# A fused retention and feed-forward kernel on one core: two units' casts and transposes moved ahead of later loads, and more zero matmuls at the start

## The chip, the core and the metric

The kernel runs on one core of a Trainium2 chip. A core has five engines, each with its own stream of instructions executed in order: TensorE (PE) for matmuls, VectorE (DVE), ScalarE (ACT), GpSimd (POOL) and SyncE (SP), which here only issues DMA transfers. Engines wait for each other and for transfers by semaphores. The metric is the device time of one execution in microseconds (us); lower is better.

## The reference

Inputs are q, k and v of shape (8 batches, 8 heads, 576 positions, 64) and two weight matrices, all float32.

```
scores = (q @ k^T) / sqrt(64)
D[h,i,j] = gamma[h] ** (i - j) if i >= j else 0      # gamma[h] = 1 - 2 ** (-5 - h)
attn = (scores * D) @ v
x = attn with heads side by side                      # 4608 tokens x 512
h = x @ w_in                                          # 512 x 2048
out = max(0.01 * h, h) @ w_out                        # 2048 x 512
```

So it is a decaying, causal linear attention with no softmax, followed by a two-layer feed-forward with a leaky rectifier, for 4608 tokens.

## The kernel before

**Two levels of tiling.** The attention works on 36 *units* of 128 tokens, each two chunks of 64. The feed-forward works on 18 *groups* of 256 tokens. Everything that goes into a matmul is float16; sums are float32 in PSUM.

**One unit.** Its k, q and v arrive by three loads of 256 KB (`loads`, L151; six half loads where a unit spans two batches). `casts(u)` (L180) makes float16 of them: `cast_k` is one ACT instruction (L157); `cast_q` and `cast_v` multiply by the decay table (L160), on DVE for units below 6 and on POOL from 6 on. Scores need q and k with the head dimension on the partitions. For units below 7, `transposes` (L187) does that with eight PE transposes and two copies out of PSUM; from unit 7 on, `cast_q` itself issues a DMA transpose from SP (L171), which reads `qk16` in SBUF and writes `qkT` in SBUF. `scores(u)` (L209) then computes the masked block's scores (L216) and the k-v products (L225) into the only `sc` PSUM tile; `masks` (L232) and `states` (L241) read it on DVE and so free it for the next unit; `state_copy` makes float16 of the state, on ACT below unit 8 and on POOL above. `outputs(u)` (L313) multiplies scores and state by v and q (L323, L334), and ACT (L342) and DVE (L346) bring the sum into `xT`.

**One group.** `g1_blocks` (L442) makes the hidden layer in eight blocks: eight matmuls of 256 columns (L454) into one of two `hps` PSUM buffers, and one ACT activation (L461), which frees the buffer. `g2_blocks` (L468) does the second layer: two token blocks of 16 matmuls of 512 columns (L477), copied out by DVE (L487) and stored by SP (L489). `g2_wide` (L508) does the same for groups 0 and 1.

**What sets the order.** The program text is each engine's order; nothing is rescheduled. The beginning is written out by hand (L542 to L654): units 0 to 7 with their casts and the first three groups' blocks between them. After that, `steady(n)` (L406) is one step: scores of unit n, outputs of n-1, masks, states, casts of n+3, and loads of n+7. `run` (L497) spreads these steps evenly between the blocks of one group's first layer and the previous group's second, so that a step's small matmuls come every few blocks.

**Queues.** Until unit 11, loads are issued by POOL, which also does casts; `ring` (L128) makes POOL wait so that only so many bytes are in flight. From unit 12 on, SP issues the loads. SP's queue thus holds, in program order, the DMA transposes, the loads from unit 12 on, and the stores of the result. Each tile of a pool has a fixed number of buffers: five for loads, six for casts and transposes.

**Zero matmuls.** `keep_warm(n)` (L377) issues n matmuls of 128x512 on a tile of zeros (L381) into an `hps` buffer that nothing reads; it stands after the PE transposes of the first units. `small_ones(60)` (L383) does it with 64x64 matmuls before the first data arrive.

Of the kernel before, what the change touches and what calls it, by code (L numbers as in the profile page):

```python
# [17 lines left out]
def kernel(  # L18
# [23 lines left out]
    nc = tc.nc  # L42
# [16 lines left out]
    NU = NT // P  # L59
# [78 lines left out]
    def load(u, x, eng):  # L138
        t = ld_pool.tile([P, H, D], FP, name=f"t32_{x}")
        t32[u, x] = t  # L140
        (b0, c0), (b1, c1) = units[u]
        src = (q, k, v)[x]
        parts = [(t, b0, c0, P)] if b0 == b1 else [(t[0:CH], b0, c0, CH), (t[CH:P], b1, c1, CH)]
        for dst, b, c, n in parts:
            if eng is nc.gpsimd:
                ring(H * n * D * 4, dst[0:1, 0, 0:1])
            eng.dma_start(  # L147
                out=dst, in_=src[b, :, CH * c : CH * c + n, :].rearrange("h t d -> t h d")
            )

    def loads(u, eng):  # L151
        for x in (1, 0, 2):
            load(u, x, eng)

    def cast_k(u):
        qk16[u] = b_pool.tile([P, 2, H, D], F16, name="qk16")
        nc.scalar.copy(out=qk16[u][:, 1], in_=t32[u, 1])  # L157

    def scaled(u, x, out):
        (nc.vector if u < NEARLY else nc.gpsimd).tensor_tensor(  # L160
            out=out,
            in0=t32[u, x],
            in1=tab_sb[:, kind(u), x // 2, :].unsqueeze(2).to_broadcast([P, H, D]),
            op=MUL,
        )

    def cast_q(u):
        scaled(u, 0, qk16[u][:, 0])
        if u >= NPE:
            qkT[u] = b_pool.tile([P, 2, NP, P], F16, name="qkT")  # L170
            nc.sync.dma_start_transpose(  # L171
                out=qkT[u].rearrange("p x c t -> p (x c) t"),
                in_=qk16[u].rearrange("t x h d -> t (x h d)"),
            )

    def cast_v(u):
        v16[u] = b_pool.tile([P, H, D], F16, name="v16")
        scaled(u, 2, v16[u])

    def casts(u):  # L180
        if u >= NU:
            return
        cast_k(u)
        cast_q(u)
        cast_v(u)

    def transposes(u, pool=None):  # L187

        qkT[u] = b_pool.tile([P, 2, NP, P], F16, name="qkT")
        if pool is None:  # L190
            trs = [y_pool.tile([P, NP, P], F16, name="yps") for x in range(2)]
        else:
            both = pool.tile([P, 2, 2 * NP, P], F16, name="sc" if pool is sc_pool else "ot")
            trs = [both[:, x, 0:NP, :] for x in range(2)]
        for x in (1, 0):
            for p in range(NP):
                nc.tensor.transpose(  # L197
                    trs[x][:, p, :],
                    qk16[u][:, x, 2 * p : 2 * p + 2, :].rearrange("t h d -> t (h d)"),
                    ident,  # L200
                )
        for x in (1, 0):
            (nc.scalar.copy if x or u < 4 else nc.vector.tensor_copy)(
                out=qkT[u][:, x], in_=trs[x]
            )
# [3 lines left out]
    def scores(u):  # L209

        a = sc_pool.tile([P, 2, 2, NP, CH], FP, name="sc")
        sc_tiles[u] = a
        for p in range(NP):
            for g in range(2):
                for j in range(2):
                    nc.tensor.matmul(  # L216
                        out=a[half(j), g, 0, p, :],
                        lhsT=qkT[u][half(g), 1, p, half(j)],
                        rhs=qkT[u][half(g), 0, p, half(j)],
                        start=True, stop=True, skip_group_check=True,  # L220
                    )
        for p in range(NP):
            for j in range(2):
                for g in range(2):
                    nc.tensor.matmul(  # L225
                        out=a[half(g), j, 1, p, :],
                        lhsT=qk16[u][half(j), 1, 2 * p + g, :],
                        rhs=v16[u][half(j), 2 * p + g, :],
                        start=True, stop=True, skip_group_check=True,
                    )  # L230

    def masks(u):  # L232
        s16s[u] = a_pool.tile([P, 2, NP, CH], F16, name="s16")
        nc.vector.tensor_tensor(  # L234
            out=s16s[u],
            in0=sc_tiles[u][:, :, 0],
            in1=mask_sb.unsqueeze(1).unsqueeze(1).to_broadcast([P, 2, NP, CH]),
            op=MUL,
        )

    def states(u, copy=True):  # L241

        st = sc_tiles[u][:, :, 1]
        s32 = a_pool.tile([P, 2, NP, CH], FP, name="s32")
        st32[u] = s32
        for j, (b, c) in enumerate(units[u]):
            if c == CB - 1:
                continue
            ends_block = c % CPB == CPB - 1
            dst = st[:, j] if ends_block else s32[:, j]  # L250
            if c == 0:
                nc.vector.tensor_copy(out=dst, in_=st[:, j])
            else:
                prev = s32[:, 0] if j else st32[u - 1][:, 1]
                nc.vector.tensor_tensor(out=dst, in0=st[:, j], in1=prev, op=ADD)  # L255
            if ends_block:
                nc.vector.tensor_tensor(
                    out=s32[:, j], in0=dst,
                    in1=gblk_sb.unsqueeze(2).to_broadcast([P, NP, CH]), op=MUL,
                )  # L260
        if copy:
            state_copy(u)
# [50 lines left out]
    def outputs(u):  # L313


        ot = ot_pool.tile([P, 2, 2 * NP, CH], FP, name="ot")
        own = ot[:, :, 0:NP]
        far = ot[:, :, NP : 2 * NP].rearrange("q r (s j) t -> q r s (j t)", j=2)
        for hp in range(NP):
            for h in (hp, hp + NP):  # L320
                o, c = divmod(h, NP)
                for j in range(2):
                    nc.tensor.matmul(  # L323
                        out=own[half(o), j, c, :],
                        lhsT=v16[u][half(j), h, :],
                        rhs=s16s[u][half(j), h % 2, h // 2, :],
                        start=True, stop=True, skip_group_check=True,
                    )
        for j in range(2):
            for s in range(2):  # L330
                for o in range(2):
                    for g in range(2):
                        p = 2 * o + s
                        nc.tensor.matmul(  # L334
                            out=far[half(o), g, s, half(j)],
                            lhsT=st_before(u, j)[half(g), p, :],
                            rhs=qkT[u][half(g), 0, p, half(j)],
                            start=True, stop=True, skip_group_check=True,
                        )
        t0 = P * u % XR  # L340
        tmp = a_pool.tile([P, NP, P], FP, name="own")
        nc.scalar.copy(  # L342
            out=tmp.rearrange("q c (j t) -> q c j t", t=CH),
            in_=own.rearrange("q j c t -> q c j t"),
        )
        nc.vector.tensor_tensor(  # L346
            out=xT[:, :, t0 : t0 + P].rearrange("q (s g) t -> q g s t", g=2),
            in0=far,
            in1=tmp.rearrange("q (s g) t -> q g s t", g=2),
            op=ADD,  # L350
        )
# [25 lines left out]
    def keep_warm(n):  # L377

        t = h_pool.tile([P, 1, TOK], FP, name="hps")
        for _ in range(n):  # L380
            nc.tensor.matmul(out=t[:, 0, :], lhsT=idle[:, 0:P], rhs=idle, start=True, stop=True)  # L381
# [24 lines left out]
    def steady(n):  # L406
        def go():
            if n < NU:
                scores(n)
            if n > NFIRST:  # L410
                outputs(n - 1)
            if n < NU:
                masks(n)
                states(n)
            casts(n + 3)
            if n + 7 < NU:
                loads(n + 7, nc.sync)

        steps.append((n - 1, go))

# [129 lines left out]
    states(0)  # L550
    cast_q(1)
    cast_v(1)
    transposes(1)
    keep_warm(1)
    cast_k(2)
    cast_q(2)
    scores(1)
# [44 lines left out]
    def more(blocks, a, b):  # L602
        for m in range(a, b):
            blocks[m]()
# [32 lines left out]
    more(g1[2], 3, 5)  # L637
    state_copy(6)
    casts(9)
    loads(12, nc.sync)  # L640
    more(g1[2], 5, 7)
    outputs(6)
    scores(7)
# [2 lines left out]
    more(g1[2], 7, 8)  # L646
    more(g2, 0, 1)
    state_copy(7)
    casts(10)
    loads(13, nc.sync)  # L650
    loads(14, nc.sync)
    more(g2, 1, 4)
    outputs(7)
    more(g2, 4, 6)  # L654
# [48 lines left out]
```

## Time and profile before

| | us |
|---|---|
| median of 6 runs | 309.73 (307.28 to 311.18) |
| the profiled execution: its own time | 311.39 |
| its span, first to last instruction | 309.6 |
| time until unit 3's first hidden-layer block on PE | 19.47 |
| DVE, ACT and POOL busy | 107.1, 137.8, 123.2 |
| PE: hidden layer (L454), second layer (L477) busy | 148.1, 128.0 |

The profile is of one execution. A row such as `L454 PE MATMUL hps<-xT,w_in` names the line in the kernel, the engine, the operation, and the tile written and those read. PEld is PE's loading of weights, beside its matmuls. SPq is SP's queue of issued transfers: the time given there is that of the issue, not of the transfer. A number in brackets is the engine's idle time just before an instruction, with what ended it. PEclk is the share of PE's full clock that was granted. The longest waits in total are of engines that follow PE:

```profile
ACT gt L461 <- PE hps L454: 130.0, 133, 2.4
DVE xT L346 <- ACT own L342: 83.9, 32, 6.3
DVE osb L487 <- PE yps L477: 75.6, 17, 6.3
POOL st L268 <- DVE s L255: 56.3, 12, 7.4
```

(Columns: who waited for whom, us in total, times, the longest.) These are waits of engines with time to spare. What PE itself waits for is small in sum, and has to be looked for by place:

```profile
PE yps L197 <- DVE qk L160: 3.0, 2, 1.6
PE sc L216 <- DMA qkT<-qk: 2.9, 1, 2.9
...
PE sc L216 <- DVE s L255: 1.2, 1, 1.2
```

### The profile page before, as it was taken

The page shows a single profiled execution, that of the slowest core. Times are in us where ns is not written, and L with a number is a line of the kernel's source. Part 1 is how long each engine was busy: PE and PEld are TensorE (multiplying, and loading weights), DVE is VectorE, ACT ScalarE, POOL GpSimd, SP SyncE. Part 2 cuts the span into 40 slices and gives each one's busy share as a digit, 9 for nine tenths or more (in the row PEclk, how much of TensorE's full clock was granted, in tenths as well). Part 3 has the DMA queues.
Part 4 walks back from the last instruction along what each step waited for, and adds up shares of the span by engine and source line. Part 5 has one row for each costly group of instructions (what it writes and reads, how often), then busy time and mean ns, then how long its engine had stood idle before and what let it go on. Part 6 is the DMA issues. An engine that isn't in the chain of part 4 may idle for free.

```text
span 309.6 us, 9470 instructions
## 1 busy us (share of the span) xinstructions
PE 295.9 (96%) x4164; PEld 199.9 (65%) x4164; DVE 107.1 (35%) x200; ACT 137.8 (45%) x240; POOL 123.2 (40%) x177
## 2 busy tenths in 40 slices
PE   4799999998699999999999999999999999999996
PEld 3468755856456666666666666766666666666663
DVE  2732035345223234333434234333334234332101
ACT  3556634846324444444444444444444444343320
POOL 8977969956333332433233333333333330000000
PEclk9999999999869999999999999999999999999999
DMA  8999997999999976887697967676873220000011
GB/s 227 248 195 229 206 274 215 227 240 204 239 209 247 238 166 170 131 212 174 170 154 186 173 174 168 173 179 173 147 199 82 78 70 36 36 36 34 36 65 70
DMA packets 120440, 50.26 MB, mean 162 GB/s; under 512 B 109264, under 2 KB 113744, under 8 KB 120400
## 3 DMA queue, kind: packets, MB, share of 16 engines
q1 hardware_dynamic: 112912, 36.38, 52.6%
q0 software_dynamic: 7056, 13.11, 18.1%
q8 instruction: 32, 0.52, 0.8%
q10 hardware_dynamic: 432, 0.17, 0.3%
q14 instruction: 8, 0.07, 0.1%
HBM read 36.81 MB, written 9.44 MB: 149 GB/s over the span
## 4 chain that ended last, share of the span: by engine, by line
PE 92%; DMA 3%; DVE 2%; issue 1%; ACT 1%; SPq 0%; POOL 0%; POOLq 0%; ACTq 0%; DVEq 0%
PE hps L454 39%; PE yps L477 35%; PE sc L216 3%; PE yps L522 2%; PE hps L522 2%; PE sc L225 2%; PE ot L323 2%; DMA t<-in_q_dram 2%; PE ot L334 1%; DMA qkT<-qk 1%; PE yps L663 1%; PE yps L197 1%; PE hps L381 1%; PE ot L290 1%; DVE s L234 1%
## 5 line engine op out<-in xcount | busy, mean ns | idle before, releaser
L454 PE MATMUL hps<-xT,w_in 128*128 128x256 f16 x1152 | 148.1, 275 | 0.0
L461 ACT ACTIVATE gt<-hps 128x512 f16<-128x512 f32 x144 | 85.8, 597 | 130.4 <-PE hps L454 130.0
L454 PEld LDWEIGHTS <-w_in 128*128 128x128 f16 x1152 | 113.1, 99 | 39.6 <-issue 1.6
L477 PE MATMUL yps<-w_out,gt 128*128 128x512 f16 x496 | 128.0, 384 | 0.0
L268 POOL CAST st<-s 128x512 f16<-128x512 f32 (+1 forms) x28 | 15.6, 556 | 144.0 <-DVE s L255 56.3
L477 PEld LDWEIGHTS <-gt 128*128 128x128 f16 x496 | 46.6, 98 | 35.1 <-issue 1.1
L346 DVE TENSOR_TENSOR xT<-ot,own 128x512 f16<-128x512 f32 x32 | 22.1, 692 | 83.9 <-ACT own L342 83.9
L487 DVE COPY osb<-yps 128x512 f32<-128x512 f32 x31 | 21.3, 687 | 75.6 <-PE yps L477 75.6
L160 POOL TENSOR_TENSOR qk<-t,cs 128x512 f16<-128x512 f32 x30 | 31.3, 1043 | 0.1
L160 POOL TENSOR_TENSOR v<-t,cs 128x512 f16<-128x512 f32 x30 | 31.2, 1042 | 0.0
L234 DVE TENSOR_TENSOR s<-sc,cs 128x512 f16<-128x512 f32 x36 | 24.6, 683 | 10.6 <-PE sc L225 10.6
L342 ACT COPY own<-ot 128x512 f32<-128x512 f32 x32 | 18.7, 585 | 11.9 <-PE ot L334 9.9
L157 ACT CAST qk<-t 128x512 f16<-128x512 f32 x36 | 22.3, 621 | 1.0 <-DMA t<-in_k_dram 1.0
L216 PEld LDWEIGHTS <-qkT 64*64 64x64 f16 x576 | 8.0, 111 | 14.0 <-issue 8.0
L255 DVE TENSOR_TENSOR s<-sc,s 128x256 f32<-128x256 f32 x40 | 16.8, 420 | 0.7
L216 PE MATMUL sc<-qkT 64*64 64x64 f16 x576 | 11.9, 203 | 4.3 <-DMA qkT<-qk 2.9
L147 POOL DMA_DIRECT2D t<-in_v_dram x13 | 11.3, 871 | 0.8 <-POOLq L687 0.8
L225 PE MATMUL sc<-v,qk 64*64 64x64 f16 x576 | 11.3, 198 | 0.0
L147 POOL DMA_DIRECT2D t<-in_q_dram x12 | 10.2, 853 | 2.1 <-DMA t<-in_k_dram 2.1
L147 POOL DMA_DIRECT2D t<-in_k_dram x12 | 10.4, 865 | 1.1 <-DMA t<-in_k_dram 1.1
L522 PEld LDWEIGHTS <-gt 128*128 128x128 f16 x64 | 5.9, 98 | 6.3
L323 PE MATMUL ot<-s,v 64*64 64x64 f16 x512 | 9.9, 195 | 0.0
(52 smaller groups left out, 147.8 us busy)
## 6 DMA issues: line engine op xcount, KB each, us to landing
out_dram<-osb SPq DMA_DIRECT2D x35, 256.0 KB, 3.5
t<-in_k_dram SPq DMA_DIRECT2D x22, 256.0 KB, 3.6
t<-in_q_dram SPq DMA_DIRECT2D x22, 256.0 KB, 3.9
t<-in_v_dram SPq DMA_DIRECT2D x21, 256.0 KB, 4.4
t<-in_v_dram POOLq DMA_DIRECT2D x11, 256.0 KB, 5.0
t<-in_k_dram POOLq DMA_DIRECT2D x10, 256.0 KB, 5.1
t<-in_q_dram POOLq DMA_DIRECT2D x10, 256.0 KB, 5.1
w_in<-in_moe_w_in_dram POOLq DMA_DIRECT2D x8, 256.0 KB, 6.9
```

The lines of the kernel that those rows point to most:

```text
L147: eng.dma_start(out=dst, in_=src[b, :, CH * c : CH * c + n, :].rearrange("h t d -> t h d"))
L157: nc.scalar.copy(out=qk16[u][:, 1], in_=t32[u, 1])
L160: (nc.vector if u < NEARLY else nc.gpsimd).tensor_tensor(out=out, in0=t32[u, x], in1=tab_sb[:, kind(u), x // 2, :].unsqueeze(2).to_broadca ...
L216: nc.tensor.matmul(out=a[half(j), g, 0, p, :], lhsT=qkT[u][half(g), 1, p, half(j)], rhs=qkT[u][half(g), 0, p, half(j)], start=True, stop=T ...
L234: nc.vector.tensor_tensor(out=s16s[u], in0=sc_tiles[u][:, :, 0], in1=mask_sb.unsqueeze(1).unsqueeze(1).to_broadcast([P, 2, NP, CH]), op=MUL,)
L342: nc.scalar.copy(out=tmp.rearrange("q c (j t) -> q c j t", t=CH), in_=own.rearrange("q j c t -> q c j t"),)
L346: nc.vector.tensor_tensor(out=xT[:, :, t0 : t0 + P].rearrange("q (s g) t -> q g s t", g=2), in0=far, in1=tmp.rearrange("q (s g) t -> q g s ...
L454: nc.tensor.matmul(out=hps[:, f, :], lhsT=w_in16[:, c, fc * P : (fc + 1) * P], rhs=xT[:, c, t0 % XR : t0 % XR + tok], start=(c == 0), stop ...
L461: nc.scalar.activation(out=g_tiles[g][:, fb * nf : (fb + 1) * nf, :], in_=hps, func=mybir.ActivationFunctionType.Lrelu,)
L477: nc.tensor.matmul(out=y_cur[g, tb], lhsT=g_tiles[g][:, f, tb * P : (tb + 1) * P], rhs=w_out16[:, f, :], start=(f == 0), stop=(f == NF - 1),)
L487: nc.vector.tensor_copy(out=osb, in_=y_cur[g, tb])
L522: nc.tensor.matmul(out=ys[n], lhsT=g_tiles[g][:, f, tb * P : (tb + 1) * P], rhs=w_out16[:, f, :], start=(f == 0), stop=(f == NF - 1),)
```

## The change

Three things change, in the hand-written order and in `steady`; no computation does.

- `casts(10)` stands right behind `casts(9)`, where `loads(12)` was, and `casts(11)` follows where `casts(10)` was; its call in step 8 goes. A DMA transpose goes with each.
- Loads 12 and 13 follow `casts(11)`; from unit 14 on, the loads are issued in step n for unit n+6 instead of n+7, so one step later.
- At the start, four zero matmuls stand on PE between `scores(0)` and the transposes of unit 1, and two instead of one behind them.

```diff
@@ steady
-            casts(n + 3)
-            if n + 7 < NU:
-                loads(n + 7, nc.sync)
+            if n + 3 > 11:
+                casts(n + 3)
+            if n + 6 < NU:
+                loads(n + 6, nc.sync)
@@ start
     cast_q(1)
     cast_v(1)
+    keep_warm(4)
     transposes(1)
-    keep_warm(1)
+    keep_warm(2)
     cast_k(2)
@@ groups 2 and 3
     more(g1[2], 3, 5)
     state_copy(6)
     casts(9)
-    loads(12, nc.sync)
+    casts(10)
     more(g1[2], 5, 7)
     outputs(6)
     scores(7)
...
     more(g2, 0, 1)
     state_copy(7)
-    casts(10)
+    casts(11)
+    loads(12, nc.sync)
     loads(13, nc.sync)
-    loads(14, nc.sync)
     more(g2, 1, 4)
     outputs(7)
```

## The prediction, made before the changed kernel ran

> **What bounds the kernel now.** I read the page's busy shares and its rows of 40 slices first, then the waits, the chain of work that ended last around the one dip, the one-microsecond windows there, and last SyncE's queue, which issues the transfers that PE waits for.
>
> ```profile
> PE 295.9 (96%) x4164; PEld 199.9 (65%) x4164; DVE 107.1 (35%) x200; ACT 137.8 (45%) x240; POOL 123.2 (40%) x177
> ...
> PE   4799999998699999999999999999999999999996
> ...
> PEclk9999999999869999999999999999999999999999
> ```
>
> PE is the bound: 96% of the span, and 92% of the chain. From 23 us to the end it has two thin slices, the 10th and 11th (70 to 85 us), and the clock dips in the 11th and 12th (77 to 93). The 10th's loss, 1.16 us before scores(10) at 74.87, ends on VectorE's state additions, which the change leaves alone. The 11th holds the real hole. The other thin place is the first 20 us. The change touches both, and nothing else could pay: a transfer or cast that moves beside a busy PE is worth nothing.
>
> ```profile
> 79.77 0.25 POOL qk L160
> 80.02 3.97 DMA qkT<-qk
> 83.99 0.04 issue
> 84.04 0.43 PE sc L216 x13
> ...
> 85.11 1.82 PE yps L477 x4
> 86.93 1.71 PE hps L454 x8
> 88.64 1.62 PE yps L477 x4
> 90.25 0.87 PE hps L454 x8
> ```
>
> This is the chain (start, us, what). PE's work before the hole ends at 81.11; scores(11) starts at 84.04, when the transpose of unit 11 has landed. PE stood 2.93 us. Behind it the same groups run at half speed until 90.25. The step that the chain puts before the transpose, a POOL cast at 79.77, is unit 13's and only happened to end then: unit 11's own cast on POOL (71.50) had ended at 72.53, and ACT's (69.47) at 70.08. What held the transpose is its queue:
>
> ```profile
> 69.33 1.57 SPq L171 DMA_TRANSPOSE qkT<-qk  x1
> 71.01 1.39 SPq L147 DMA_DIRECT2D t<-in_k_dram  x2
> 72.51 2.03 SPq L147 DMA_DIRECT2D t<-in_q_dram  x2
> 74.63 1.27 SPq L147 DMA_DIRECT2D t<-in_v_dram  x2
> 76.01 0.57 SPq L147 DMA_DIRECT2D t<-in_k_dram  x1
> 76.67 0.54 SPq L147 DMA_DIRECT2D t<-in_q_dram  x1
> 77.30 1.73 SPq L147 DMA_DIRECT2D t<-in_v_dram  x1
> 79.12 0.73 SPq L489 DMA_DIRECT2D out_dram<-osb  x1
> ```
>
> Unit 10's transpose, then nine loads of units 13 and 14 and one store, and only at 80.02 unit 11's. SP issues in order, without a pause, so a transpose that was ready at 72.53 left 7.5 us late.
>
> **The change part by part.** (a) *Transpose 11 ahead of the loads.* casts(11) now follows casts(10), and both precede loads(12). On POOL the four multiplies of 9 and 10 run 62.00 to 66.03, then it idles 5.10 us; q(11) fits there, 66.0 to 67.05. On ACT unit 11's cast takes the place that unit 10's had (64.86). On SP: T9 ends its issue at 66.59, T10 follows at once (it was 69.33, behind loads(12)), T11 some 1.3 to 3 us later (the issues of T8 to T13 took 1.43 to 3.12), so about 68.5, landing with the 3.6 to 4.0 of T10 and T11 at about 72.5. PE asks at 81.1, so the 2.93 us go, with 8 us to spare.
>
> (b) *The clock behind the hole.* Row first: windows of 1 us (us, busy, instructions, PEclk, DMA share, GB/s):
>
> ```profile
> 81.00:82.00 1.00, 0.11 (x1) 1.00 0.96 284
> 82.00:83.00 1.00, 0.00 (x0) 1.00 1.17 139
> 83.00:84.00 1.00, 0.00 (x0) 0.60 1.16 245
> 84.00:85.00 1.00, 0.96 (x64) 0.50 1.24 280
> ```
>
> PEclk is 0.50 from about 83.2 to 90.04. The pieces from 84.04 to 90.25 take 6.22 us; the same kinds at full clock a step later (92.86 on: small matmuls 0.64, then 0.97, 0.87 and 0.86) take 3.34. So 2.88 us more. The Trainium skill, "TensorE: Matmul & The Clock Gate", Part 1, says that the half clock comes after at least one idle window of about 3.4 us; a hole of 2.93 us would then cost 2.93 and no more. In this trace a hole of 2.93 us did drop the clock, so I take the trace: 5.81 us, against 2.93 by the rule. But the page's windows run freely, so that another execution may lose less; the rule's figure stays as the small end.
>
> (c) *What (a) puts in front.* casts(10) now precedes the last three blocks of group 2 in ACT's order. ACT has its k casts 9 and 10 in a row, 0.52 more ahead of the activation at 60.57. That one ended at 61.17 and PE's next block took its buffer at 61.36: slack 0.19, so PE waits 0.33 us. Bounds 0 and 0.52.
>
> (d) *Loads later.* Loads(12), three DMAs, are moved behind T10 and T11: the k part leaves at 69.5 to 70.2 instead of 66.70 and lands 3.6 later, 73.1 to 73.8; its cast on ACT was at 72.50 with the activations queued behind it (73.02). So ACT waits some 0.6 to 1.0. PE's next block needs the first of these buffers at 75.70, and it is free by 74.9: hidden. Loads(13), six half DMAs, start at about 72 and land at 76 to 77, for a cast that was at 76.36: ACT late by 0 to 0.5, and PE's block at 78.32 covers it. The store is next. Loads(14) leave about 78, land by 82, needed after scores(11), 82.4. T12 then issues at about 80 to 81.5 and lands by 85.5; PE wants it about 5.8 us after scores(11), at 87. Value 0; from below no gain, as no PE wait names a load; from above 1.5 (both ACT waits a microsecond longer). In the rest of the run every unit's loads go out one step later: three steps (some 23 us, at 7.7 a unit: 93.4 to 108.8 for two) remain for landings of 3.6 to 4.4. Nothing.
>
> (e) *Zero matmuls at the start.* PE does scores(0) until 8.85, four transposes at 8.78, waits 1.65 for DVE's cast of q(1), does four more at 11.04. The four zero matmuls, at the 0.43 that L381 takes here (half speed), fill 8.85 to 10.55; the first four transposes end at 11.1 instead of 9.4. ACT's copy of them was at 10.95, behind a state cast, so it moves 0.2; the second keep_warm adds one more 0.43, to 12.5, where scores(1) began at 12.33. Cost about 0.25 us. Is there a gain? The matmuls up to about 22 us go at half speed (thirteen of L454 from 19.47 in 2.71 us, 0.21 each, against 0.11 later), whatever the PEclk row says there. The same page, Part 1, wants about 3.4 us of sustained work and, in Part 4, does not count transposes as such. The four and the two zeros are 1.7 and 0.85 us with transposes between: by the rule not enough. By the trace: from 15.6 to 18.4 PE was nearly always busy with 64x64 matmuls and transposes and did not speed up. So no gain; the bound is minus 2.7 (first hidden-layer block held to 17.82, when its second weight part landed, instead of 19.47: 1.65; its sixteen matmuls at 1.73 instead of 2.83: 1.1). Even then scores(8) at 68.87 waits for the transpose of unit 8, landed at 68.59, which POOL's cast at 60.00 sets: 0.3 of slack. I take +0.25.
>
> Sum: -2.93 - 2.88 + 0.33 + 0.25 = -5.2. The profiled execution took 311.39 (span 309.6): 306.2. It is 1.7 above the median of 309.73, and part of that is likely a longer clock loss than most runs have. With 1.2 to 2.9 of it, the median becomes 309.73 - 2.93 - (1.2 to 2.9) + 0.58 = 304.5 to 306.2. I predict 305.5.
>
> **The rivals.** *Only the hole goes* (19%): most runs do not lose the clock, as the rule has it; 309.73 - 2.93 + 0.58 = 307.4. For: the runs spread over 3.9 us. Against: the windows above.
>
> *The start speeds up* (15%): the zeros open the clock a window earlier; 0.3 to 2 us off, 303.5 to 305. For: the hole of 1.65 us is filled. Against: the transposes between, and unit 8's landing.
>
> *The next transpose is late* (9%): T12 now stands behind loads 12 to 14. It must land by 87. The queue from 71 to 80 took 0.9 us a DMA; with five more microseconds of backlog PE stands some 2 us at scores(12): 307.5 to 308.5.
>
> *ACT starves PE, slower* (7%): the casts of k(12) and k(13) sit in ACT's order ahead of the activations that free PE's two buffers. It decides when k(12) lands after about 74.5 (75.70 less a cast spacing of 0.5 and an activation of 0.6): from there each microsecond is one of PE. At 77.5 the hole is 3 us and drops the clock again: -5.81 + 3 + 2.88 + 0.58 = +0.7, and with k(13) as late, +2 to +4: 310.5 to 313.5. Against: it needs landings of 7 us, as only T8 and T9 had, behind the four stores of 57 to 61 us.
>
> That the order does not change as said is excluded: the instruction order of both shows T10 and T11 ahead of loads(12).
>
> **How the numbers follow.** The forecast has the remaining 50%. The range is 303.0 to 308.5: below lies the full early start (4%), above the starved ACT and a bad T12 (10%). Within 1% means 306.6 to 312.8, about what a measurement of this kernel can tell from no change. Faster: nearly all of the forecast (46), the early start (15), a part of the other two (6): 0.67. Slower: the worse half of the starved ACT, 0.04. The rest, 0.29.
>
> **What would show it.** Right: T11 issued near 68.5 us and landed before 75; scores(11) with no wait on qkT; PEclk 9 in slices 11 and 12; PE idle in 80 to 100 us under 0.3 instead of 2.93; the k casts of 12 and 13 on ACT ended by DMA, but PE's blocks behind them on time. For (c), L454 some 0.3 late at 61.4. For (e), L381 at 0.43 each and L454 at half speed until about 22. Wrong: a PE wait over 1 us at scores(8) to scores(13), a second dip of PEclk, or the same dip elsewhere.

## The result and the profile after

The changed kernel takes 305.42 us (median of 18 runs, 303.88 to 308.38) against 309.29 for the kernel before (37 runs): a ratio of 0.989, 95% interval 0.9865 to 0.9915. Medians take all runs; the ratios, here and below, leave out those over 1.5% above the fastest of the same kernel. The profiled execution of the changed kernel took 304.47 with a span of 302.6; before it was 311.39 and 309.6. The two profiles thus differ by 7 us, nearly twice what the medians do, and part of the work below is to say why. (In the changed kernel, lines behind the edit at L415 stand one or two further down: L454 is L455, L477 is L478. In what is shown, `...` stands for lines left out.)

The page's busy row, and its PE and clock rows in 40 slices:

```profile
PE 291.6 (96%) x4169; PEld 197.2 (65%) x4169; DVE 107.0 (35%) x200; ACT 137.9 (46%) x240; POOL 122.4 (40%) x177
...
PE   5889999898999999999999999999999999999996
...
PEclk9999999999999999999999999999999999999999
```

PE's busy time fell by 4.3 us although five matmuls more are recorded. 2.7 of it lie between scores(8) and scores(12): the dip of the clock in slices 11 and 12 is gone, and matmuls that ran at half speed don't any more. The other 1.6 lie ahead of scores(8), where the clock opens earlier. What changed on SP, in order of time (start, us, instruction):

```profile
55.71 2.92 SPq L534 DMA_DIRECT2D out_dram<-osb  x4
59.37 8.79 SPq L171 DMA_TRANSPOSE qkT<-qk  x4
68.27 0.52 SPq L147 DMA_DIRECT2D t<-in_k_dram  x1
...
76.10 0.58 SPq L490 DMA_DIRECT2D out_dram<-osb  x1
76.78 1.45 SPq L147 DMA_DIRECT2D t<-in_k_dram  x1
78.33 0.53 SPq L147 DMA_DIRECT2D t<-in_q_dram  x1
78.95 1.19 SPq L147 DMA_DIRECT2D t<-in_v_dram  x1
80.31 1.63 SPq L171 DMA_TRANSPOSE qkT<-qk  x1
```

The transposes of units 8 to 11 leave in a row; unit 11's is issued at 66.5 and has landed at 70.2. From issue to landing it took 3.6 us, where it was 4.0 before: the transfer is not faster, it leaves earlier. Unit 12's goes out at 80.31, lands at 85.1, and PE asks at 85.82, so there are 0.7 us to spare. On PE, around the place of the old hole:

```profile
58.34 0.30 PE L334 MATMUL ot<-qkT,st 64*64 64x64 f16 x16
59.57 0.32 PE L216 MATMUL sc<-qkT 64*64 64x64 f16 x16 [0.93 <-DMA qkT<-qk]
...
77.15 2.78 PE L455 MATMUL hps<-xT,w_in 128*128 128x256 f16 x24
79.86 0.32 PE L216 MATMUL sc<-qkT 64*64 64x64 f16 x16
...
85.82 0.32 PE L216 MATMUL sc<-qkT 64*64 64x64 f16 x16
```

scores(11) at 79.86 and scores(12) at 85.82 wait for nothing. A smaller wait of 0.93 us is new, at scores(7), for the transpose of unit 7. From scores(12) to the end both kernels take 216.8 us, so every difference lies before it. Comparing the two executions at milestones on PE:

| us | before | after | lead |
|---|---|---|---|
| first hidden-layer block | 19.47 | 17.81 | 1.66 |
| scores(3) | 22.44 | 19.64 | 2.80 |
| scores(8) | 68.87 | 67.46 | 1.41 |
| scores(11) | 84.04 | 79.86 | 4.18 |
| scores(12) | 92.79 | 85.82 | 6.97 |

So there are three pieces: a quicker start, half of which is lost again by scores(8), 0.93 of it in the new wait at scores(7); the hole, 2.8; and the slow clock behind it, 2.8.

### The profile page after: what moved, and what is told of

It reads as the page before. It is cut to its first block, busy times and chain, and to the rows that moved or that the text cites. A ratio compares the mean times of both kernels' runs of the same rounds, so it can differ in the third digit from the quotient of the medians.

```text
span 302.6 us, 9480 instructions
## 1 busy us (share of the span) xinstructions
PE 291.6 (96%) x4169; PEld 197.2 (65%) x4169; DVE 107.0 (35%) x200; ACT 137.9 (46%) x240; POOL 122.4 (40%) x177
## 3 DMA queue, kind: packets, MB, share of 16 engines
q1 hardware_dynamic: 112912, 36.38, 54.3%
## 4 chain that ended last, share of the span: by engine, by line
PE 74%; POOL 11%; DMA 9%; issue 4%; SPq 2%; ACT 0%; POOLq 0%; ACTq 0%
PE yps L478 34%; PE hps L455 33%; POOL t L147 5%; DMA t<-in_k_dram 4%; DMA w_out<-in_moe_w_out_dram 3%; DMA w_in<-in_moe_w_in_dram 2%; PE sc L216 2%; POOL v L160 2%; POOL qk L160 2%; POOL probe L132 1%; PE ot L323 1%; PE yps L665 1%; PE ot L334 1%; SPq L147 1%; PE sc L225 1%
## 5 line engine op out<-in xcount | busy, mean ns | idle before, releaser
L455 PE MATMUL hps<-xT,w_in 128*128 128x256 f16 x1152 | 146.0, 273 | 1.2 <-ACT st L268 0.9
L455 PEld LDWEIGHTS <-w_in 128*128 128x128 f16 x1152 | 112.0, 98 | 39.5 <-issue 2.0
L478 PE MATMUL yps<-w_out,gt 128*128 128x512 f16 x496 | 126.3, 380 | 0.0
L478 PEld LDWEIGHTS <-gt 128*128 128x128 f16 x496 | 46.3, 98 | 34.3
```

The costliest lines, as they stand in the source:

```text
L455: nc.tensor.matmul(out=hps[:, f, :], lhsT=w_in16[:, c, fc * P : (fc + 1) * P], rhs=xT[:, c, t0 % XR : t0 % XR + tok], start=(c == 0), stop ...
L478: nc.tensor.matmul(out=y_cur[g, tb], lhsT=g_tiles[g][:, f, tb * P : (tb + 1) * P], rhs=w_out16[:, f, :], start=(f == 0), stop=(f == NF - 1),)
```

## The experiments

Three causes can stand behind the gain: the hole with its clock loss, the zero matmuls at the start, or an accident of the two executions that were profiled. And of the order, three things moved at once: two casts, their transposes, and the loads. Each ratio is against the kernel before on the same chip. All keep the computation as it is; the zero matmuls write a buffer that nothing reads.

**The order alone** is the changed kernel with the start of before.

```diff
-    keep_warm(4)
     transposes(1)
-    keep_warm(2)
+    keep_warm(1)
```

> The new order of casts, transposes and loads, with the start as before (one zero matmul). Theory A (the hole at scores(11) is the gain, and the start adds its own 1.4 us): the hole is gone and the clock stays; PE runs at half speed until about 22 us as before; 306 to 307 us against 309.3, a ratio of 0.990 to 0.993. Theory B (the order alone makes the gain, the start only shifts waits): 305.4, ratio 0.986 to 0.989. Theory C (the start alone makes the gain, since most executions of the kernel before have no clock loss): no faster than 308.5, ratio over 0.997.

305.93 us, ratio 0.9877 (0.9839 to 0.9915); the mean clock in all six of its runs was at least 0.999. The ratio lies in the bounds of B, though its interval reaches into those of A: the order makes the gain, or nearly all of it.

**The zeros alone** is the reverse.

```diff
+    keep_warm(4)
     transposes(1)
-    keep_warm(1)
+    keep_warm(2)
```

> The zero matmuls of the change alone, the order as before. Theory A: the clock opens near 11 us instead of 22, PE reaches unit 3's first hidden-layer block 1 to 2 us earlier, but unit 11's transpose leaves SP no earlier, so the hole at scores(11) grows by what the start gained: ratio 0.997 to 1.003, and PE's wait there is 4 us or more. Theory C: ratio 0.985 to 0.99. If the zeros do not open the clock: ratio 1.000 to 1.002, and L454 at 0.21 us a matmul until about 22 us.

310.0 us, ratio 0.9979 (0.995 to 1.0009). The zeros did open the clock early, at 9.3 us, and PE reached scores(3) at 20.13. It was at the hole at 79.13, 2 us earlier than before, but unit 11's transpose left SP only 1.3 us earlier, at 78.72:

```profile
82.55 0.32 PE L216 MATMUL sc<-qkT 64*64 64x64 f16 x16 [3.42 <-DMA qkT<-qk]
```

The wait was 3.42 us instead of 2.93, less than the 4 expected. A start gained in front of a transfer that is late anyway makes a longer wait. Of these 22 runs, 19 show a mean clock under full; this profile is one of the other three.

**The kernel before, once more**, unchanged.

> The kernel before once more, unchanged, for a second look at one execution: is the hole at scores(11) there each time, and does the clock fall behind it each time? Theory A: the hole is there, 2 to 4 us, and the ratio is 1.000 within 0.003. If the hole is missing here, the profile of before was a rare one and the prediction was right by chance.

310.53 us, ratio 1.0024 (0.9987 to 1.0061). The hole is there again, and the clock falls behind it, but for one stretch of 3.41 us where the first profile had 6.83:

```profile
83.32 0.32 PE L216 MATMUL sc<-qkT 64*64 64x64 f16 x16 [3.14 <-DMA qkT<-qk]
...
84.89 1.91 PE L454 MATMUL hps<-xT,w_in 128*128 128x256 f16 x8
86.60 1.82 PE L477 MATMUL yps<-w_out,gt 128*128 128x512 f16 x4
88.25 1.04 PE L454 MATMUL hps<-xT,w_in 128*128 128x256 f16 x8
```

The clock of every run tells how typical this is. Of the 81 runs of the kernel before that stand beside these experiments, on two chips, the mean clock was 1.00 in 28 (mean time 308.3 us), 0.994 in 39 (310.1) and 0.989 in 14 (311.5). Half the clock for 3.41 us of some 308 makes a mean of 0.994, so these are no, one or two stretches, at 1.8 and 1.4 us each. (The 14 runs of this experiment: 2, 9 and 3.) The profile of before was one with two. That is most of what it had over the median.

**The casts moved, the loads not.** Units 10 and 11 are cast and transposed early as in the change, but the loads keep their distance of seven units.

```diff
-            casts(n + 3)
+            if n + 3 > 11:
+                casts(n + 3)
@@
     casts(9)
-    loads(12, nc.sync)
+    casts(10)
@@
-    casts(10)
+    casts(11)
+    loads(12, nc.sync)
     loads(13, nc.sync)
     loads(14, nc.sync)
```

> Casts and transposes of units 10 and 11 ahead of loads 12 to 14, but the loads at their old distance (unit n+7 in step n; loads 12, 13 and 14 together), and the start as before. If the two casts are what matters, as predicted: the same as the new order alone within 0.002, unit 11's transpose issued before 70 us. If the shorter distance of the loads matters: unit 12's transpose stands behind four units of loads, PE waits for it 1 to 4 us at scores(12), and most of the gain is lost: ratio 0.997 or more.

308.97 us, ratio 0.9972 (0.9935 to 1.0008): most of the gain is gone, eight of 14 runs lost clock, and it can be seen where. PE, and its windows of 1 us (us, busy, instructions, PEclk, DMA share, GB/s):

```profile
82.13 0.32 PE L216 MATMUL sc<-qkT 64*64 64x64 f16 x16
...
87.12 1.04 PE L455 MATMUL hps<-xT,w_in 128*128 128x256 f16 x8
90.32 0.32 PE L216 MATMUL sc<-qkT 64*64 64x64 f16 x16 [2.16 <-DMA qkT<-qk]
...
91.16 1.89 PE L478 MATMUL yps<-w_out,gt 128*128 128x512 f16 x4
```

```profile
89.00:90.00 1.00, 0.00 (x0) 1.00 0.87 189
90.00:91.00 1.00, 0.68 (x64) 0.80 1.17 263
91.00:92.00 1.00, 1.00 (x21) 0.50 1.14 258
```

scores(11) at 82.13 is free of its wait, and scores(12) has inherited it, with the drop: unit 12's transpose now stands behind four units of loads (issued 85.25, landed 90.3). The hole moved one step on.

**The loads later, the casts not.** This is the other half.

```diff
-            if n + 7 < NU:
-                loads(n + 7, nc.sync)
+            if n + 6 < NU:
+                loads(n + 6, nc.sync)
@@
-    loads(14, nc.sync)
```

> Only the loads one step later (unit n+6 in step n, no loads of unit 14 by hand); casts 10 and 11 and the start as before. Unit 11's transpose then stands behind loads 12 and 13 and one store, but no more behind loads 14. Theory A (three loads are what the queue holds too many): it leaves SP near 77 us instead of 80, lands just before PE asks at 81; the hole is under 0.8 us, no clock loss: ratio 0.988 to 0.992, nearly all of the gain without moving a cast. Rival (the transpose must be ahead of loads 12 and 13 as well): a hole of 1.5 us or more stays, ratio 0.994 or more.

305.98 us, ratio 0.9881 (0.983 to 0.9931), and the clock was 1.00 in all six runs. Unit 11's transpose left at 78.03, and what remains of the hole is short, and leaves the clock alone:

```profile
82.90 0.32 PE L216 MATMUL sc<-qkT 64*64 64x64 f16 x16 [0.88 <-DMA qkT<-qk]
```

In this execution, the slowest of the six, PE came to the place at 82.02, 0.9 later than in the profile of before; had it come as early, the wait would have been longer. But none of the six runs lost clock. The loads from unit 14 on issued one step later thus bring the whole gain; the moved casts bring none that these runs can tell beside it.

**The hole filled** leaves everything of before in its place, and only keeps PE busy while it waits.

```diff
+            if n == 11:
+                keep_warm(13)
             if n < NU:
                 scores(n)
```

> The kernel before with 13 zero matmuls of 128x512 (0.216 us each, 2.8 us) on PE ahead of scores(11): they stand where PE waits for unit 11's transpose and make nothing earlier. It separates the two terms of the hole. If the clock loss behind the hole is a cost of its own (2.88 us in the profiled execution of before, 0.7 windows of 1.7 us on average over its runs): no execution drops below full clock, and the time falls by 0.8 to 1.5 us, ratio 0.995 to 0.9975. If the drop costs nothing that the wait has not cost already: ratio 1.000 or above. If filling takes all of the gain: 0.989.

308.42 us beside 310.13, ratio 0.9969 (0.9944 to 0.9993); 18 of 22 runs kept the full clock, where it was 7 of 27 before. PE in the profile (L477 is L479 here):

```profile
79.52 2.97 PE L381 MATMUL hps<-idle 128*128 128x512 f16 x13
82.68 0.32 PE L216 MATMUL sc<-qkT 64*64 64x64 f16 x16 [0.19 <-DMA qkT<-qk]
...
83.32 1.04 PE L479 MATMUL yps<-w_out,gt 128*128 128x512 f16 x4
```

So the clock loss is a cost of its own: about 1.7 us in the median, 1.0 by the ratio, whose interval allows 0.2 to 1.7. The filled hole brings the median to where the runs of before that kept the full clock are, 308.3. The rest of the gain, some 2.4 to the 305.98 of the loads alone, is the wait.

**The transposes of units 7 and 8 sooner.** In the changed kernel PE waits for unit 7's. POOL casts it behind the issue of loads; here the casts go first.

```diff
-    loads(10, nc.gpsimd)
     casts(7)
+    loads(10, nc.gpsimd)
@@
-    loads(11, nc.gpsimd)
     casts(8)
+    loads(11, nc.gpsimd)
```

> The change, and on top of it casts(7) ahead of loads(10) and casts(8) ahead of loads(11) on POOL, so that the transposes of units 7 and 8 leave some 2 to 3 us earlier. In the changed kernel PE waits 0.93 us at scores(7) for unit 7's transpose. If the start's gain is lost there: that wait goes and the time falls by 0.5 to 1 us against the changed kernel, 304.5 to 305, ratio 0.985 to 0.988. If the wait only moves to unit 8 or 9, or unit 11's loads become late: the same as the changed kernel.

306.19 us, ratio 0.9899 (0.985 to 0.9948), beside the changed kernel's 0.9891: no gain. Unit 7's transpose landed at 54.3, and the wait at scores(7) went. Unit 8's left 3 us earlier than in the changed kernel's profile, at 56.42, but landed at 66.6, where it was 66.7. And ACT waited 3.10 and 1.61 us for k(12) and k(13), so that PE waited 1.1 and 0.92 us for activations at 74 and 78 us.

**The changed kernel again**, twice, beside the others.

> The changed kernel once more, on the chip of these runs, to stand beside the others: ratio 0.987 to 0.991, no wait of PE for a transpose from scores(8) to scores(13), no dip of the clock.

> The changed kernel beside the three others on their chip: ratio 0.987 to 0.991; scores(8) within 1 us of the landing of unit 8's transpose.

0.9891 (0.984 to 0.9942) and 0.9847 (0.9804 to 0.9891). The first one's profile, without the wait at scores(7), shows what the early cast of k(10) costs:

```profile
59.50 1.03 PE L455 MATMUL hps<-xT,w_in 128*128 128x256 f16 x8 [0.31 <-ACT gt L462]
```

The second is an execution that lost its lead; by their mean clock of 0.989 to 0.994, five of the changed kernel's 30 runs lost clock somewhere. scores(8) came 1.8 us after unit 8's transpose, not within 1, since the loss lay ahead of it:

```profile
58.52 0.30 PE L334 MATMUL ot<-qkT,st 64*64 64x64 f16 x16
61.40 0.43 PE L216 MATMUL sc<-qkT 64*64 64x64 f16 x16 [2.58 <-DMA qkT<-qk]
...
61.97 1.89 PE L455 MATMUL hps<-xT,w_in 128*128 128x256 f16 x8
```

It is the same fault at unit 7: a late transpose, a hole of 2.58, half clock behind it.

**The stores held back.** Unit 8's transpose takes 7 us behind the four stores of groups 0 and 1.

```diff
-tc.tile_pool(name="op", bufs=4)
+tc.tile_pool(name="op", bufs=6)
@@ g2_wide
-                nc.sync.dma_start(out=out[r0 : r0 + P, :], in_=osb)
+                held.append((out[r0 : r0 + P, :], osb))
@@
     casts(9)
+    for to, osb in held:
+        nc.sync.dma_start(out=to, in_=osb)
     casts(10)
```

> The change, and the four stores of groups 0 and 1 held back on SP until behind the transposes of units 8 and 9 (six store buffers instead of four, so that nothing waits for them). In the looks so far unit 8's transpose takes 7 us from issue to landing behind these stores, and scores(8) follows its landing by 0 to 0.9 us. If that landing caps what a quicker start can bring: unit 8's transpose lands by 64 us, PE waits for no transpose from unit 7 to 13, and the time is 0.5 to 1.5 us under the changed kernel beside it, ratio 0.983 to 0.987. If not: the same as the changed kernel, ratio 0.987 to 0.991.

305.2 us, ratio 0.9879 (0.9833 to 0.9925): not told apart from the changed kernel. PE waited for unit 7's transpose alone, 0.16 us. So these runs do not show that the landing of unit 8's behind the stores caps the gain.

**The order alone, again.**

> The new order without the new zero matmuls, once more, beside the changed kernel on one chip. If the zeros bring what the earlier clock brings at unit 3 (up to 2.8 us): 1.5 us or more over the changed kernel. If it is swallowed before scores(8), as the looks so far suggest: within 0.6 us of it, ratio 0.987 to 0.992.

305.97 us, ratio 0.9878 (0.9838 to 0.9918). The ratio is as expected if the zeros bring nothing; but the changed kernel beside it took 304.47, 1.5 us less, which was the bound for a gain. Earlier, on the same chip, the changed kernel had 306.41. Over all its runs the order alone has a mean of 305.88 (12 runs), the changed kernel 305.51 (30 runs). If the new zeros bring anything in the end, it is some 0.4 us by these means; these runs do not settle it.

**Only casts(11) moved.** Loads 12 stay ahead of casts(10).

```diff
     casts(9)
-    casts(10)
+    loads(12, nc.sync)
@@
-    casts(11)
-    loads(12, nc.sync)
+    casts(10)
+    casts(11)
     loads(13, nc.sync)
```

> The change with one cast less moved: loads(12) stay ahead of casts(10), as before, and casts(10) and casts(11) follow together ahead of loads(13). The 0.33 us that PE loses to ACT's early cast of k(10), and the late k(12), should go; unit 11's transpose leaves SP at about 70 us, soon enough. If both are real costs: 0.3 us under the changed kernel, ratio 0.986 to 0.990. If they are hidden: the same within 0.002.

304.25 us, the lowest median of all, ratio 0.9823 (0.9785 to 0.9861), under the 0.986 to 0.990 expected. PE's wait behind k(10) is gone, and k(12) is cast on time (70.78, with no wait); scores(10) waits for unit 10's transpose instead of DVE, 1.47 us where it was 1.16. It is better than the changed kernel beside it (304.47) by no more than the intervals allow, so that it may be as good rather than better.

## Why the prediction was right, and where it was not

The forecast of 305.5 us met 305.42, and the sum held because its two large terms did: the hole and the clock loss are real, and both go. That the number is so close is partly luck: one step was given to the wrong part of the change, one was wrong, and the clock loss was put into the median at about 1.9 (307.4 less 305.5), between the ends of a wide range.

**The hole (-2.93).** It is in every profile of the kernel before (2.93, 3.14) and of the zeros alone (3.42), and the time falls when it goes. But the step that books it under (a), the transpose ahead of the loads, gives it to the wrong part of the change. Moving the casts without the loads only handed the hole to scores(12), while the loads one step later, which (d) put at 0 with "no gain, as no PE wait names a load", did it alone. The wait names the transpose, and the transpose stood behind the loads: the loads were the cost, as the prediction's own lines of SP show, and it did not draw that conclusion for the edit in `steady`. The rival of a late next transpose is what happens without that edit: 2.16 us, where it said some 2.

**The clock (-2.88 in the profile, 1.2 to 2.9 in the median).** Filling the hole gave 1.7 in the median, within the range, and 1.0 by the ratio, just under it. The rule of the Trainium skill ("TensorE: Matmul & The Clock Gate", Part 1), half the clock after an idle window of about 3.4 us, would have said 307.4; here holes of 2.16 to 3.14 us dropped the clock. The trace was the better guide, but one trace was not enough: it was an execution with two slow stretches, and what made the number right was to take about 1.9 for the median and not the whole 2.88.

**ACT's early cast (+0.33).** Measured 0.31 where no other wait stood in front of it.

**Later loads beside ACT (0).** k(12) and k(13) waited 0.72 and 0.93 us in the profile after, as expected or a little more:

```profile
71.91 0.62 ACT L157 CAST qk<-t 128x512 f16<-128x512 f32 x1 [0.72 <-DMA t<-in_k_dram]
...
75.99 0.62 ACT L157 CAST qk<-t 128x512 f16<-128x512 f32 x1 [0.93 <-DMA t<-in_k_dram]
```

PE's blocks behind them came on time. With the casts of units 7 and 8 moved as well, they no longer did: the rival of a starved ACT, with 1.1 and 0.92 us. (Its counter-argument misreads one landing: of the transposes of units 8 and 9 only the first took over 7 us, 7.5; the other took 5.9.)

**The start (+0.25).** This step is wrong. It said that the clock does not open earlier; it opened at 10.86 us instead of 21.77. (That is where the trace's records of the clock begin and where the matmuls become faster; PEclk shows 9 before it too.) Before, and then after:

```profile
18.19 1.49 PE L381 MATMUL hps<-idle 128*128 128x512 f16 x3
19.47 3.03 PE L454 MATMUL hps<-xT,w_in 128*128 128x256 f16 x16
```

```profile
7.93 1.89 PE L381 MATMUL hps<-idle 128*128 128x512 f16 x4
9.61 1.18 PE L197 MATMUL yps<-ident,qk 128*128 128x128 f16 x8
10.59 0.73 PE L381 MATMUL hps<-idle 128*128 128x512 f16 x2
...
17.81 1.91 PE L455 MATMUL hps<-xT,w_in 128*128 128x256 f16 x16 [0.95 <-ACT st L268]
```

The first four zero matmuls take 0.43 each, the last two 0.35 and 0.22, and sixteen of the hidden layer take 1.91 instead of 3.03. The lead at scores(3), 2.80 us (0.86 of it because q of unit 0 landed sooner), is the bound of 2.7 that the step named. The step also held that scores(8) would take the lead away, waiting for unit 8's transpose until 68.59. In this pair that failed: the transpose landed at 66.7, and scores(8) came 1.41 us earlier. But it came at 67.47 in the second profile of the kernel before too, without new zeros, so the 1.41 cannot be put down to them. Neither an earlier transpose of unit 7 nor stores held back brought time, so what takes the rest of the lead over the runs is not shown. Of the rival, 0.3 to 2 us off, there remain the 0.4 that are not settled.

## What to carry over

When an engine waits for a transfer, look at what its queue sent between the moment it was ready and the moment it was issued; here taking transfers out helped, and moving the late one ahead did not by itself: it passed the place at the queue's tail to the next one. A gain ahead of a wait that ends on a late transfer was worth nothing while that wait stood. And when one profile lies off the median, count in the other runs how often its costly event happens before its size is used.

## What was not expected of the hardware

The drop of the clock came with much less than 3.41 us idle. In the traces' records of the clock, the half-speed stretches between matmuls last 3.41 or 6.83 us, and the stretches at full clock ahead of them last 51.2 to 68.27, which is 15 to 20 times 3.41; so the clock seems to be judged in intervals of 3.41, counted from its opening. PE's idle time within the interval that ends at each drop was 2.10 us in the first profile of before, 1.95 in the second, 2.16 with the casts alone, 2.11 in the third profile of the changed kernel. In the zeros alone, a hole of 3.42 us lay across two intervals, 1.85 in one and 1.57 in the other (counted from the opening at 9.30), and the clock did not fall. Between 1.85 and 1.95 us idle of 3.41 lies the border in these five cases, and here a hole of 2 to 3.4 us dropped the clock or did not by where it lay.

A few zero matmuls open the clock far sooner than their own length suggests. In the seven profiles of kernels with the new zeros it was open at 9.0 to 13.3 us, in the seven without at 16.4 to 22.4, though these are only five matmuls more, of six that stand around eight transposes and take some 2.4 us in all. How much of an interval has to be filled, and with what, these runs do not show.
